# Four v tiles first, projections in independent pairs, and parts of LN moved to GpSimd, in a fused attention and token-MLP kernel

## The chip, the cores and the metric

The kernel runs on one core of one Trainium2 chip. The time is the device time of one execution in microseconds (us), as a median of several executions. Most executions of one kernel agree within about 1 us (the kernel before took 178.03 to 179.87 us over all rounds; one execution in e6 fell into a slow state and took 217 us); more about that spread below. A profile is one execution with the hardware profiler on; its span (first to last instruction) is about 1.7 us shorter than the time. Names of engines in the profile: PE is TensorE's matmul side, PEld its weight loads, DVE is VectorE, ACT is ScalarE, POOL is GpSimd, SP is the engine that issues most DMAs. "PEclk" is the share of TensorE's full clock that the throttle granted.

## The reference, cut to what matters

Two branches of the same sequence (2048 tokens, 448 features) are mixed by a gate.

```python
def _layernorm(x, axis=-1, eps=1e-05):
    m = jnp.mean(x, axis=axis, keepdims=True)
    v = jnp.var(x, axis=axis, keepdims=True)
    return (x - m) / jnp.sqrt(v + eps)

# branch A: 16 heads of 28; q, k, v = x @ wq, x @ wk, x @ wv; 4 segments of 512 tokens, causal
# attention inside a segment, a linear memory (elu+1 features) over earlier segments; then @ wo
# branch B, a token MLP:
h = _layernorm(x)                                   # 16 tiles of 128 tokens x 448
u = gelu(einsum('bsd,sf->bdf', h, w1) + b1)         # f = 1792
y = einsum('bdf,fs->bds', u, w2) + b2
out = g * a + (1 - g) * y.transpose(0, 2, 1)        # g = sigmoid((x * gate_w).sum(-1))
```

## The kernel before

The program is one straight list of operations. Each has a name, its reads and writes, and possibly an alternative engine; a table `ORDER` fixes which engine runs it and in which order. Semaphores are derived from the reads and writes. Every engine works strictly down its own list, so an operation that is late holds up all that stand behind it.

The names used below: `trx0_*` are TensorE transposes of the first x tiles and `xTcp*` their copies out of PSUM; `v01a` to `d`, `k0`, `q0`, ... are projections; `padk*`, `padq*` copy wk and wq into a padded layout; `sc0_0` is a group of score matmuls, `exp0_0` its exponential on ScalarE, `mask0_*` its causal mask on GpSimd; `pv0` multiplies the first masked probabilities with v; `u0-5` is the matmul of hidden tile 0 with x tile 5, so it waits for `ln5`; `y15` is the last output tile.

```python
def ln_coef(t):                       # one call for 4 tiles
    t4 = slice(t, t + 4)
    op("DVE", lambda e: e.tensor_scalar_add(vpe[:, t4], mv[:, t4, 1], 1e-5), ...)               # variance + eps
    op("POOL", lambda e: e.tensor_tensor(rstd[:, t4], vpe[:, t4], mhalf[:, t4], op=ALU.pow), ...)  # ** -0.5
    op("DVE", lambda e: e.scalar_tensor_tensor(nmr[:, t4], mv[:, t4, 0], -1.0, rstd[:, t4],
                                               op0=ALU.mult, op1=ALU.mult), ...)                # -mean * rstd

def ln_apply(t):                      # 128 x 448, bf16, in place
    op("DVE", lambda e: e.tensor_scalar(xh[:, t, :], xh[:, t, :], rstd[:, t : t + 1], nmr[:, t : t + 1],
                                        op0=ALU.mult, op1=ALU.add), ...)                        # x * rstd + nmr

# project(): four outputs a, b, c, d; each pair shares the array as two half-row tiles
a, b, c, d = outs
R_h = Res(name, psum=True)            # ties the four parts together
ab = part(name + "a", (run(a, 0, True), run(b, 1, True)), ())
cd = part(name + "b", (run(c, 0, True), run(d, 1, True)), ())
part(name + "c", (run(b, 0, False), run(a, 1, False)), ()).deps.append(ab)
part(name + "d", (run(d, 0, False), run(c, 1, False)), uses).deps.append(cd)
...                                   # cut
ORDER = {"PE": """ warm fill0 gtr ... trx0_1 fill5 ... v01a v01b v01c v01d k0a k0b k0c k0d q0a ... sc0_4 pv0
                   u0-0 u4-0:2 u0-1:2 u1-0 ... y15-13 y12-10:4 """,            # cut
         "POOL": """ id0 z3_0 id1 v0 z3_1 mhalf v1 mask0_0_0 rstd0 rstd8 mask0_1_1 mask0_1_3 mask0_2_2
                     mask0_2_2~2 rstd4 maskg0 rstd12 ... """}                   # cut
```

## Time and profile before

The median was 178.05 us. What matters:

| | before |
|---|---|
| span of the profile | 176.6 us |
| useful matmuls, estimate from start-to-start distances (189 ns per 448 columns, 216 ns per pair of 512) | 157.4 us |
| first useful matmul / last one ends | 6.54 / 173.66 us |
| pv0 starts | 26.93 us |
| one LN apply on VectorE | 0.39 us |

First the page's lines of busy time and of the granted clock in 40 slices. PE is the engine with the least room, and it is dense from the second slice to the last; GpSimd has plenty.

```profile
span 176.6 us, 3765 instructions
PE 169.1 (96%) x1460; PEld 81.9 (46%) x1468; DVE 150.7 (85%) x332; ACT 128.8 (73%) x159; POOL 67.3 (38%) x93
...
PE   8899899999999999999999989999999999999993
...
PEclk9999999999999999999999999999999999999999
```

The chain of waits that ended last, by engine, is mostly TensorE itself:

```profile
PE 72%; DVE 15%; ACT 6%; DMA 2%; issue 1%; SPq 1%; POOL 1%; ACTq 0%
```

### The profile page before, as it was taken

Reading aid. Unit: us, or ns where it says so; the run is one execution under the profiler, and the core shown is the slowest. Engines: PE = TensorE matmul, PEld = TensorE weight load, DVE = VectorE, ACT = ScalarE, POOL = GpSimd, SP = SyncE. Lnnn points to the kernel's source line nnn. Section 1 sums busy time; section 2 is a strip of 40 time slices with the busy share of each in tenths; the row PEclk is TensorE's granted clock in tenths of the full one; section 3 lists DMA queues with packets and bytes.
Section 4 is the critical chain, followed back from the end, with each engine's and each line's share of the span. In section 5 each row is a group of like instructions: output and inputs, shape, how many; then the busy total and the mean of one; then the engine's idle time right before and its main releaser. Section 6 shows DMA issues by size and latency. Waiting matters only on the chain.

```text
span 176.6 us, 3765 instructions
## 1 busy us (share of the span) xinstructions
PE 169.1 (96%) x1460; PEld 81.9 (46%) x1468; DVE 150.7 (85%) x332; ACT 128.8 (73%) x159; POOL 67.3 (38%) x93
## 2 busy tenths in 40 slices
PE   8899899999999999999999989999999999999993
PEld 2654244443444444454444544444544445555561
DVE  0689999999988999998999898999999998994204
ACT  2559998889997899989999999997476795001100
POOL 7000853263153700383170560089527765220000
PEclk9999999999999999999999999999999999999999
DMA  5999992328899429922136450012910591909012
GB/s 146 347 273 315 290 233 44 84 59 227 144 245 258 118 61 277 261 11 43 28 80 167 102 151 0 7 30 66 264 41 0 176 265 36 280 6 266 20 52 78
DMA packets 49729, 24.51 MB, mean 139 GB/s; under 512 B 14240, under 2 KB 49472, under 8 KB 49712
## 3 DMA queue, kind: packets, MB, share of 16 engines
q1 hardware_dynamic: 49560, 24.16, 54.5%
q8 instruction: 11, 0.18, 0.4%
q10 hardware_dynamic: 152, 0.12, 0.2%
q14 instruction: 6, 0.05, 0.1%
HBM read 18.76 MB, written 2.36 MB: 120 GB/s over the span
## 4 chain that ended last, share of the span: by engine, by line
PE 72%; DVE 15%; ACT 6%; DMA 2%; issue 1%; SPq 1%; POOL 1%; ACTq 0%
PE t L1071 25%; PE t L672 15%; PE t L1042 14%; PE t L1022 7%; PE t L934 6%; ACT t L943 4%; PE t L971 4%; DMA t<-in_A_wk_dram 2%; DVE t L893 2%; PE t L820 2%; DVE t L708 1%; ACT t L1046 1%; DVE t L1054 1%; DVE t L754 1%; DVE t L779 1%
## 5 line engine op out<-in xcount | busy, mean ns | idle before, releaser
L943 ACT ACTIVATE t<-t 128x2048 bf16<-128x2048 f32 x40 | 75.1, 1876 | 7.9 <-PE t L934 7.7
L946 POOL TENSOR_SCALAR_AFFINE_SELECT t<-t 128x512 bf16<-128x512 bf16 x64 | 44.4, 714 | 51.8 <-ACT t L943 51.2
L1042 PE MATMUL t<-t 128*128 128x448 bf16 x224 | 46.9, 353 | 0.3
L1071 PE MATMUL t<-t 128*128 128x448 bf16 (+2 forms) x238 | 46.5, 342 | 0.2
L672 PE MATMUL t<-t 64*128 64x512 bf16 (+3 forms) x336 | 34.8, 350 | 2.5 <-DVE t L720 0.7
L1071 PEld LDWEIGHTS t<-t 128*128 128x128 bf16 x238 | 21.7, 98 | 20.4 <-issue 2.5
L1042 PEld LDWEIGHTS t<-t 128*128 128x128 bf16 x224 | 20.2, 98 | 21.4 <-issue 3.4
L1002 POOL TENSOR_TENSOR t<-t 128x448 bf16<-128x448 f32 x12 | 14.5, 1210 | 33.5 <-DVE t L998 15.4
L672 PEld LDWEIGHTS t<-t 64*128 64x128 bf16 x336 | 17.4, 94 | 17.4 <-DVE t L877 1.3
L1028 ACT ACTIVATE t<-t 128x448 bf16<-128x448 f32 x11 | 8.0, 728 | 17.5 <-PE t L1022 17.5
L1076 DVE SCALAR_TENSOR_TENSOR t<-t 128x448 bf16<-128x448 f32 (+2 forms) x17 | 10.7, 640 | 8.4 <-PE t L1071 8.3
L934 PE MATMUL t<-t 28*128 28x512 bf16 (+3 forms) x256 | 15.8, 301 | 0.6 <-ACT t L943 0.4
L1022 PE MATMUL t<-t 128*128 128x448 bf16 x64 | 14.4, 353 | 0.1
L1008 DVE STREAM_TRANSPOSE t<-t 128x512 bf16<-128x512 bf16 x16 | 11.0, 693 | 0.5 <-POOL t L1002 0.4
L934 PEld LDWEIGHTS t<-t 28*128 28x128 bf16 x256 | 4.4, 92 | 14.9 <-ACT t L943 7.7
L987 DVE STREAM_TRANSPOSE t<-t 128x512 f32<-128x512 f32 x16 | 11.0, 699 | 0.3 <-PE t L971 0.2
L971 PE MATMUL t<-t 128*32 128x512 bf16 (+3 forms) x256 | 10.9, 301 | 0.0
L1059 DVE SCALAR_TENSOR_TENSOR t<-t 128x448 bf16<-128x448 f32 x14 | 9.2, 664 | 1.2 <-ACT t L1057 1.1
L1046 ACT ACTIVATE t<-t 128x448 f32<-128x448 f32 x14 | 8.9, 638 | 1.7 <-PE t L971 1.0
L877 DVE BATCH_NORM_STATS2 t<-t 128x6 f32<-128x448 bf16 x16 | 9.6, 613 | 0.3 <-DMA t<-in_A_x_dram 0.3
L1054 DVE SCALAR_TENSOR_TENSOR t<-t 128x448 f32<-128x448 f32 x14 | 9.2, 665 | 0.0
L998 DVE SCALAR_TENSOR_TENSOR t<-t 128x448 f32<-128x448 f32 x12 | 8.9, 740 | 0.1
(77 smaller groups left out, 184.8 us busy)
## 6 DMA issues: line engine op xcount, KB each, us to landing
t<-in_B_w_dram SPq DMA_DIRECT2D x7, 1024.0 KB, 6.6
t<-in_B_w_dram SPq DMA_DIRECT2D x8, 896.0 KB, 5.5
out_dram<-t SPq DMA_DIRECT2D x15, 112.0 KB, 4.4
t<-in_A_x_dram SPq DMA_DIRECT2D x3, 448.0 KB, 5.0
t<-in_A_wo_dram SPq DMA_DIRECT2D x4, 98.0 KB
t<-in_A_wv_dram SPq DMA_DIRECT2D x1, 336.0 KB, 4.1
t<-in_A_wk_dram SPq DMA_DIRECT2D x1, 336.0 KB, 4.1
t<-in_A_wq_dram SPq DMA_DIRECT2D x1, 336.0 KB, 4.5
```

Source lines behind the costliest of these rows:

```text
L672: last = e.matmul(bank(o["b"])[:, 0 : o["n"]], o["w"](r, c), o["x"](r, c), start=first, stop=end, skip_group_check=True)
L934: last = e.matmul(bank(hl)[:, c0 : c0 + w], kT[r, hg, s * 512 + j * 128 : s * 512 + j * 128 + 128], qT[r, hg, s * 512 + 128 * j : s * 512 ...
L943: op("ACT", lambda e: e.activation(pslot(g), ps[:, 0:4, :], ACT.Exp, scale=SCALE), reads=R_bank[0:4], writes=[g.res], take=g, name=f"exp{p ...
L946: op("POOL", lambda e, c0=c0: e.affine_select(pslot(g)[:, :, c0 : c0 + 128], pslot(g)[:, :, c0 : c0 + 128], pattern=[[0, 4], [1, 128]], co ...
L971: last = e.matmul(bank(cb)[32 * hl : 32 * hl + 32, 128 * j : 512], vaug[:, 4 * s + j, 32 * h : 32 * h + 32], pslot(P_fill[u // 2][f])[:, h ...
L987: dv(lambda e: e.transpose(t2[:, 0, :], bank(cb)[:, 0:512]), [bres(cb)], [R_tt[tb][0]], "ta", 630, use=(cb,))
L1002: op("POOL", lambda e: e.tensor_tensor(o3, n3[0], n3[1], op=ALU.add), reads=R_tt[tb], writes=[R_ob[tb]], name=f"o{u}", cost=1280, port=Tru ...
L1008: dv(lambda e: e.transpose(oT[:, hg, s * 512 : s * 512 + 512], o), [R_ob[tb]], qres(hg, s), "ot", 635)
L1022: last = e.matmul(bank(b)[:, 0:D], oT[:, hg, T * 128 : T * 128 + 128], wo_sb[:, hg, :], start=(hg == 0), stop=(hg == NHG - 1), skip_group_ ...
L1042: op("PE", lambda e, st=st: e.matmul(bank(b)[:, 0:D], w1c[:, st, f2 * 128 : f2 * 128 + 128], xh[:, st, :], start=(st == 0), stop=(st == NT ...
L1054: op("DVE", lambda e: e.scalar_tensor_tensor(gg[:, q, :], gg[:, q, :], 1.0, vh[:, q, :], op0=ALU.add, op1=ALU.mult), reads=[R_gg[q], R_vh[ ...
L1071: op("PE", lambda e, ft=ft: e.matmul(bank(b)[:, 0 : c1 - c0], w2c[:, ft, t2_ * 128 : t2_ * 128 + 128], uT[:, ft, c0:c1], start=(ft == 0), ...
```

## The change

Its intent: fill TensorE's early wait for the padded wk with work that needs only wv (four whole v tiles instead of two in halves); load wv in three pieces, so that the first matmuls need only two of them; let pairs of outputs finish independently; and relieve VectorE in the crowded first 40 us by giving 8 of 16 LN applies, the small pads and the addition of eps to GpSimd. LN becomes subtract-multiply, which saves the small `nmr` instruction. All engines get a new order, and the warm-up matmuls are fewer.

```diff
-    load_w(lambda: wvx, WV, R_wv, "wv", ("SP", "SP"))
+    op("SP", lambda e: e.dma_start(wvx[:, 3, 0:D], WV[320:448]), writes=[R_wv[0]], name="ldwv0", ...)
+    for k, c, n in ((1, 0, 1), (2, 1, 2)): ...            # chunk 0, then chunks 1 and 2
-    warm_up(7, "warm", -1)                                # and NFILL = 9
+    warm_up(5, "warm", -1)                                # and NFILL = 6
+        for k in range(0, len(outs), 2):                  # project(): independent pairs
+            a, b = outs[k : k + 2]
+            whole = run(a, 0, True), run(b, 1, True)
+            if cut and k == 0:                            # the part that needs two pieces of wv only
+                part(name + "s", [seq[0:2] for seq in whole], (), R_wv[0:2])
+                whole = [seq[2:] for seq in whole]
 ... (cut)
     def ln_coef(t):
-        op("DVE", ... tensor_scalar_add(vpe[:, t4], mv[:, t4, 1], 1e-5) ...)
-        op("POOL", ... rstd = vpe ** -0.5 ...)
-        op("DVE", ... nmr = mean * -1.0 * rstd ...)
+        op("POOL", lambda e: e.tensor_scalar(rstd[:, t4], mv[:, t4, 1], 1e-5, None, op0=ALU.add), ...)
+        op("POOL", ... rstd = rstd ** -0.5 ...)
     def ln_apply(t):
-        op("DVE", lambda e: e.tensor_scalar(xh[:, t, :], xh[:, t, :], rstd[:, t : t + 1], nmr[:, t : t + 1],
-                                            op0=ALU.mult, op1=ALU.add), ...)
+        def fn(e):
+            return e.tensor_scalar(xh[:, t, :], xh[:, t, :], mv[:, t, 0:1], rstd[:, t : t + 1],
+                                   op0=ALU.subtract, op1=ALU.mult)
+        op("DVE", fn, ..., alt=("POOL", fn, pool_cost(448)))
 ... (cut) ORDER, GpSimd's list:
+        ... padx1 padk1 padq1 padq0 vpe0 rstd0 padq3 ln0 mask0_0_0 ln2 vpe4 rstd4 mask0_1_1
+        ln4 ln6 ln1 mask0_1_3 mask0_2_2 mask0_2_2~2 ln5 mask0_3_0 maskg0 vpe8 rstd8 mask0_4_1 ln7 vpe12 rstd12 ln10 ...
 ... TensorE's list ends with the 128-column half of y15 instead of y12-10:4:
-        ... y15-13~2 y15-13 y12-10:4
+        ... y14-13 y12-9:5 y15-0~2 ... y15-13~2
```

`pool_cost(448)` is the estimate for one LN apply on GpSimd; it gives 0.55 us.

## The prediction

> **What bounds the kernel.** TensorE. The page's busy line gives PE 96% of 176.6 us (VectorE 85%) at full granted clock, and the chain of waits that ended last is 72% PE. Matmul records carry latency (353 ns), so I took start-to-start distances on the timeline: 189 ns per 448-column matmul, 216 ns per 512-column pair of half-row projections. That makes 157.4 us of useful matmuls between 6.54 and 173.7 us, so about 9 us are not streaming. About half of those are changes of tiling: a matmul before a score group takes 285, not 189 ns. The Trainium skill, "TensorEngine Tiling (Array Packing)", Key Properties, says that a change of mode drains the array; this trace agrees, some 0.1 us each. Both orders have nearly as many changes (96 and 94), so that half stays.
>
> **What the change can reach.**
> 1. *Start.* v01 begins at 6.54 us, after ScalarE's second copy of transposed x (ends 6.46) and the last wv piece (lands 6.41). ScalarE's x tile is now issued 0.25 us earlier and only half of wv is needed first: -0.2 us.
> 2. *k0.* Before: v01 is used up at 7.9 us and k0 starts at 8.63, because the padded wk is ready only then (0.74 us lost). Now four v tiles come first, 14 pairs x 0.19 = 2.7 us, until about 9.0; wk lands about 0.6 us later than its 7.3 us because wv goes first; padk0 (0.55 us) and padx0 (0.2 us) follow, so k0 can start at about 9. Work due anyway fills the gap: -0.6 us.
> 3. *14 to 24 us.* Stalls before sc0_0, around the bias transpose and before k1 and q1 sum to 1.6 us, waits for evacuations by a VectorE busy with statistics. Pairs release banks after two outputs instead of four, statistics start near 3.5 instead of 6.8 us, and some 4 us of VectorE work go to GpSimd (8 of 16 LN applies at 0.3 us, small pads 1.0 us, eight 0.08 us coefficient instructions). I expect half: -0.8 us.
> 4. *Middle, 27 to 150 us.* Dense, with about 1.8 us of single stalls: -0.2 us, either sign.
> 5. *Tail.* The last matmul is followed by a 448-column final (0.68 us) and its 112 KB store, landing 2.4 us after it; after the change by 128 columns (0.35 us) and 32 KB: -0.5 us.
>
> **What it adds.** GpSimd, idle from 4 to 17.7 us, gets pads and LN applies. An LN apply there should take 0.6 us (a 512-column mask takes 0.64), but masks next to VectorE's two-input float operations took 0.93 to 1.1 us. The Trainium skill, "GPSIMD Engine Reference", Specifications, tells of SBUF interfaces shared with VectorE; those masks agree. LN applies precede masks in GpSimd's order, so pv0 may come up to 1 us late.
>
> **Sum.** About -2.3 us: 175.7 us, range 173.9 to 177.3. Faster by over 2%: 0.18, within 2%: 0.79, slower by over 2%: 0.03.
>
> **What would show it.** First v matmul near 6.3 us; no gap before k0; four v tiles done by 9.1; fewer PE gaps between 13 and 24 us; LN applies on GpSimd of 0.6 to 1.0 us; pv0 about 1 to 2 us earlier than 26.9; span after the last matmul 2.4 instead of 2.9 us.
>
> **What would make it wrong.** wk or wq landing over 1 us later; GpSimd LN over 1.2 us, delaying masks and u0; a later full clock, as there is less warm-up; the new order paying elsewhere in the dense middle.

## More of the kernel before

The group of all LN applies, with its columns: line, engine, operation, tiles, shapes, count, then busy us and mean ns of one, then idle time before them.

```profile
L893 DVE TENSOR_SCALAR t<-t 128x448 bf16<-128x448 bf16 x16 | 5.7, 389 | 0.1
```

And TensorE's timeline (start us, length us, engine, line, operation, shapes, count, idle time before and what ended it) around pv0, line L971. There is no gap ahead of it, and the first MLP matmuls (L1042) follow at once.

```profile
26.60 0.40 PE L934 MATMUL t<-t 28*128 28x384 bf16 x8
26.93 0.73 PE L971 MATMUL t<-t 128*32 128x512 bf16 x16
27.59 3.58 PE L1042 MATMUL t<-t 128*128 128x448 bf16 x18
```

## The result, and the profile after

The changed kernel took 183.64 us (183.27 to 184.42 in 4 runs) against 178.1 us for the kernel before in the same rounds: slower by 3.1% (ratio 1.0307, 95% interval 1.026 to 1.0354). Ratios here and below are the mean time of one kernel's fast runs over that of the other's of the same rounds, so they are not quite the ratios of the medians.

The lines that answer to those of before:

```profile
span 182.7 us, 3702 instructions
PE 170.8 (94%) x1435; PEld 80.5 (44%) x1435; DVE 148.2 (81%) x313; ACT 127.4 (70%) x153; POOL 83.8 (46%) x110
...
PE   7799980998999999999999999999999999999994
...
PEclk9999999699999999999999999999999999999999
...
PE 63%; POOL 12%; ACT 9%; DVE 8%; DMA 3%; issue 2%; SPq 2%; ACTq 0%
```

There is a hole in PE's row: a slice of 0 around 28 to 32 us. Right after it the granted clock dips, and GpSimd has gone from 1% to 12% of the chain that ended last. The group of LN applies on GpSimd, then its timeline and TensorE's at the hole:

```profile
L894 POOL TENSOR_SCALAR t<-t 128x448 bf16<-128x448 bf16 x8 | 15.2, 1902 | 0.0
```

```profile
24.08 0.63 POOL L949 TENSOR_SCALAR_AFFINE_SELECT t<-t 128x512 bf16<-128x512 bf16 x1
24.71 5.55 POOL L894 TENSOR_SCALAR t<-t 128x448 bf16<-128x448 bf16 x3
30.22 1.93 POOL L949 TENSOR_SCALAR_AFFINE_SELECT t<-t 128x512 bf16<-128x512 bf16 x3
```

```profile
25.63 1.47 PE L678 MATMUL t<-t 64*128 64x512 bf16 x12
32.20 1.26 PE L974 MATMUL t<-t 128*32 128x512 bf16 x16 [5.11 <-POOL t L949]
33.39 0.61 PE L937 MATMUL t<-t 28*128 28x384 bf16 x8
33.94 2.50 PE L1045 MATMUL t<-t 128*128 128x448 bf16 x8
```

One LN apply on GpSimd takes 1.90 us, not 0.6. Three of them in a row (`ln4 ln6 ln1`, 5.55 us) stand in front of the three masks that pv0 needs. TensorE idles for 5.11 us until the last of them is done. Then the throttle halves its clock: in a view by stretches, 26.3 to 32.2, 32.2 to 35.6 and 35.6 to 42.4 us, with the columns length, busy us and instructions of each engine, granted clock, DMA share and GB/s:

```profile
26.30:32.20 5.90, 0.80 (x8) 0.21 (x4) 2.94 (x9) 2.42 (x4) 5.83 (x7) 1.00 0.98 212
32.20:35.60 3.40, 3.40 (x29) 1.32 (x30) 1.41 (x3) 1.55 (x1) 3.32 (x5) 0.50 0.15 45
35.60:42.40 6.80, 6.15 (x40) 2.41 (x37) 4.69 (x16) 4.83 (x7) 6.71 (x7) 1.00 0.08 29
```

From pv0's stall on, GpSimd is busy nearly all the time. Where the extra time is by the traces: the first u matmul starts at 33.94 instead of 27.59 us (+6.35), and the last matmul ends at 180.30 instead of 173.66 us (+6.64). So against the kernel before nearly all of it has been lost by 34 us. (Against e1 below, which has the change's own TensorE order, the two differences are 5.14 and 6.93 us: there, 1.8 us of the loss comes after 34 us.)

The head did not gain either. The last piece of wk landed at 9.51 us (before: 7.32), and k0 started at 10.27 us (before: 8.63):

```profile
9.53 0.69 DVE L620 COPY t<-t 128x1176 bf16<-128x1176 bf16 x2 [2.85 <-DMA t<-in_A_wk_dram]
```

### The profile page after: what moved, and what is told of

Its sections match the earlier page's. It is cut to its first block, busy times and chain, and to the rows that moved or that the text cites. A ratio compares the mean times of both kernels' runs of the same rounds, so it can differ in the third digit from the quotient of the medians.

```text
span 182.7 us, 3702 instructions
## 1 busy us (share of the span) xinstructions
PE 170.8 (94%) x1435; PEld 80.5 (44%) x1435; DVE 148.2 (81%) x313; ACT 127.4 (70%) x153; POOL 83.8 (46%) x110
## 4 chain that ended last, share of the span: by engine, by line
PE 63%; POOL 12%; ACT 9%; DVE 8%; DMA 3%; issue 2%; SPq 2%; ACTq 0%
PE t L1074 24%; PE t L678 11%; PE t L1045 10%; POOL t L894 7%; PE t L1025 7%; ACT t L946 5%; PE t L937 5%; PE t L974 4%; DMA t<-in_A_wk_dram 3%; POOL t L949 2%; POOL t L889 2%; ACT t L1049 1%; PE t L960 1%; ACT t L1060 1%; DVE t L1062 1%
## 5 line engine op out<-in xcount | busy, mean ns | idle before, releaser
L949 POOL TENSOR_SCALAR_AFFINE_SELECT t<-t 128x512 bf16<-128x512 bf16 x64 | 43.1, 691 | 51.3 <-ACT t L946 50.6
L1045 PE MATMUL t<-t 128*128 128x448 bf16 x224 | 48.0, 358 | 0.7 <-POOL t L894 0.6
L678 PE MATMUL t<-t 64*128 64x512 bf16 (+1 forms) x308 | 35.1, 367 | 2.1 <-DMA t<-in_A_wv_dram 0.8
L678 PEld LDWEIGHTS t<-t 64*128 64x128 bf16 x308 | 15.5, 94 | 19.3 <-issue 3.2
L1031 ACT ACTIVATE t<-t 128x448 bf16<-128x448 f32 x10 | 7.2, 727 | 16.1 <-PE t L1025 16.1
L974 PE MATMUL t<-t 128*32 128x512 bf16 (+3 forms) x256 | 11.4, 312 | 5.1 <-POOL t L949 5.1
L894 POOL TENSOR_SCALAR t<-t 128x448 bf16<-128x448 bf16 x8 | 15.2, 1902 | 0.0
L990 DVE STREAM_TRANSPOSE t<-t 128x512 f32<-128x512 f32 x16 | 11.0, 702 | 4.8 <-PE t L974 4.7
L1025 PE MATMUL t<-t 128*128 128x448 bf16 x64 | 14.2, 353 | 0.0
L974 PEld LDWEIGHTS t<-t 128*32 128x32 bf16 x256 | 5.7, 98 | 11.7 <-POOL t L949 5.8
L988 DVE STREAM_TRANSPOSE t<-t 128x512 f32<-128x512 f32 x12 | 8.5, 705 | 1.4 <-PE t L960 1.4
```

The lines of the kernel that those rows point to most:

```text
L678: last = e.matmul(bank(o["b"])[:, 0 : o["n"]], o["w"](r, c), o["x"](r, c), start=first, stop=end, skip_group_check=True)
L894: return e.tensor_scalar(xh[:, t, :], xh[:, t, :], mv[:, t, 0:1], rstd[:, t : t + 1], op0=ALU.subtract, op1=ALU.mult)
L949: op("POOL", lambda e, c0=c0: e.affine_select(pslot(g)[:, :, c0 : c0 + 128], pslot(g)[:, :, c0 : c0 + 128], pattern=[[0, 4], [1, 128]], co ...
L974: last = e.matmul(bank(cb)[32 * hl : 32 * hl + 32, 128 * j : 512], vaug[:, 4 * s + j, 32 * h : 32 * h + 32], pslot(P_fill[u // 2][f])[:, h ...
L990: dv(lambda e: e.transpose(t2[:, 0, :], bank(cb)[:, 0:512]), [bres(cb)], [R_tt[tb][0]], "ta", 630, use=(cb,))
L1025: last = e.matmul(bank(b)[:, 0:D], oT[:, hg, T * 128 : T * 128 + 128], wo_sb[:, hg, :], start=(hg == 0), stop=(hg == NHG - 1), skip_group_ ...
```

## The experiments

Theory A: the LN applies on GpSimd, at 1.9 us each, hold up masks and tiles; this costs the 6 us. Rival B: the new order of projections and loads costs it, since wk lands 2.2 us later. Rival C: less warm-up lowers the clock. Edits of `ORDER` are shown as the names that moved; everything unnamed is as in the kernel it starts from.

### e1_ln_dve: the 8 LN applies back on VectorE

```diff
 POOL: - ln0 ln2 ln4 ln6 ln1 ln5 ln7 ln10
 DVE:  ... cpq1_3 + ln0 ln1 ln2 ... cpq1_0 cpq1_2 + ln4 ln5 ... bna14 + ln6 ln7 ta0 ... ln9 + ln10 ...
```

> The changed kernel with one edit: its 8 LN applies on GpSimd are given back to VectorE, all else kept. Theory A (GpSimd's LN applies of 1.87 us each hold up the masks, so pv0 starts at 32.2 instead of 26.9 us and TensorE's granted clock drops while it waits): pv0 back to about 27.2, no stall of over 1 us before it, granted clock 1.00, time 177 to 178.5 us. Rival B (the new order of projections and loads, with wk landing 2.2 us later, is what costs): over 181 us, since those stay. Rival C (less warm-up lowers the clock): clock stays under 1.00.

Measured: 177.51 us, 0.9941 of the kernel before (0.9912 to 0.9971), with the clock at 1.00. The whole loss is gone, and the rest of the change is a small gain. pv0 started at 27.82 us; it now waited 1.26 us, for VectorE:

```profile
25.09 1.47 PE L680 MATMUL t<-t 64*128 64x512 bf16 x12
27.82 0.73 PE L976 MATMUL t<-t 128*32 128x512 bf16 x16 [1.26 <-DVE t L775]
```

Rivals B and C fall as causes of the loss: the order of projections and loads and the short warm-up are all still there (wk landed at 8.98 us). A's figure for pv0 was 0.6 us too good, because of that wait; its "no stall of over 1 us" was a miss too.

### e2_masks_first: the masks of pv0 ahead of five LN applies, all on GpSimd

```diff
 POOL: ... ln0 mask0_0_0 - ln2 vpe4 rstd4 mask0_1_1 - ln4 ln6 ln1 mask0_1_3 mask0_2_2 mask0_2_2~2
       + ln1 ln2 ln4 ln5 ln6 mask0_3_0 ...
```

> The changed kernel with GpSimd's order alone altered: the four masks that pv0 waits for go ahead of ln1, ln2, ln4, ln5 and ln6, which then follow one another. If it is only the place of the masks in GpSimd's order (theory A1): about 178 us, pv0 at about 27. If it is GpSimd's total work before the first MLP tiles (theory A2, 8 x 1.87 = 15 us): pv0 at about 27 but the u matmuls then wait for ln1 to ln6, ready every 1.9 us until about 36, and the time stays above 180.5 us.

Measured: 186.5 us, 1.0438 of the kernel before, so even slower than the change. pv0 starts at 27.36 us, but the u matmuls then wait for one LN apply after the other; the last line is of the view of all waits (us in total, times, longest us):

```profile
30.14 0.93 PE L1046 MATMUL t<-t 128*128 128x448 bf16 x4 [0.86 <-POOL t L895]
31.00 0.18 PE L855 MATMUL t<-t 30*128 30x30 bf16 x1
31.99 0.36 PE L1046 MATMUL t<-t 128*128 128x448 bf16 x1 [0.80 <-POOL t L895]
33.83 2.05 PE L1046 MATMUL t<-t 128*128 128x448 bf16 x5 [1.48 <-POOL t L895]
...
39.68 0.35 PE L1046 MATMUL t<-t 128*128 128x448 bf16 x1 [2.34 <-DVE t L860]
...
DVE t L895 <- POOL t L890: 8.9, 2, 7.6
```

The clock record of this run has two stretches of 3.4 us at half clock (from 33.5 and from 40.3 us) instead of one. The longest wait, 2.34 us, is for a small VectorE operation (L860), but it too goes back to GpSimd: VectorE had stood idle for 7.6 us until GpSimd, behind five LN applies, computed the `rstd` (L890) of the next four tiles. So it is not the place of the masks alone; 15 us of LN do not fit on GpSimd before the MLP starts. Moving the wait only broke it into pieces. Whether the second stretch at half clock adds to the 2.3% over the change was not tried.

### e3_forms: what one LN apply costs on GpSimd, in eight forms

```diff
 def ln_apply(t), on GpSimd:
+    ln0: tensor_scalar(x, mean, rstd, subtract, mult)      ln2: tensor_scalar(x, rstd, mean, mult, add)
+    ln4: tensor_scalar(x, 0.001, 1.5, subtract, mult)      ln6: tensor_scalar(x, rstd, mult)
+    ln1: as ln0, 224 columns     ln5: tensor_scalar(x, 1.5, mult)
+    ln7: tensor_copy(x)          ln10: tensor_tensor(x, x, mult)
```

> The changed kernel with its 8 LN applies on GpSimd written in 8 forms, with a wrong result on purpose, to measure what one costs: ln0 as is (1.87 us), ln2 multiply-add with two columns, ln4 subtract-multiply with two constants, ln6 multiply by one column, ln1 as is on 224 columns, ln5 multiply by one constant, ln7 a copy, ln10 a product of two tensors. If the cost is per element and per arithmetic step (theory): half the columns about 1.0 us, one step about 1.0 to 1.2, two constants no cheaper than two columns, copy about 0.6. If it is a fixed cost of fetching columns: 224 columns near 1.8 us and two constants about 0.6.

Measured, in the order ln0, ln4, ln6, ln5, ln1, ln10, ln2, ln7:

```profile
L909 POOL TENSOR_SCALAR t<-t 128x448 bf16<-128x448 bf16 x1 | 1.9, 1875 | 0.0
L898 POOL TENSOR_SCALAR t<-t 128x448 bf16<-128x448 bf16 x1 | 1.7, 1720 | 0.1
L900 POOL TENSOR_SCALAR t<-t 128x448 bf16<-128x448 bf16 x1 | 1.5, 1453 | 0.0
L904 POOL TENSOR_SCALAR t<-t 128x448 bf16<-128x448 bf16 x1 | 1.3, 1340 | 0.0
L902 POOL TENSOR_SCALAR t<-t 128x224 bf16<-128x224 bf16 x1 | 1.1, 1117 | 0.0
...
L908 POOL TENSOR_TENSOR t<-t 128x448 bf16<-128x448 bf16 x1 | 0.9, 932 | 0.0
...
L896 POOL TENSOR_SCALAR t<-t 128x448 bf16<-128x448 bf16 x1 | 0.7, 714 | 0.0
L906 POOL COPY t<-t 128x448 bf16<-128x448 bf16 x1 | 0.6, 588 | 0.0
```

The per-element part of the theory held: 224 columns fewer save 0.76 us, and constants save only 0.15 us against columns. What nobody expected is in the line before the last: multiply-add with two columns, the form that the kernel before used, took 0.71 us, less than half of a multiplication alone (1.45 us). Why is not shown. My own "one step 1.0 to 1.2 us" was too low. So the change did two things at once to LN: it moved half of the applies, and it rewrote all of them into a form that costs nothing on VectorE (0.39 us either way, the median of 16 in the kernel before and in e1) and 2.6 times as much on GpSimd. One record of each form is thin evidence; e5 gives eight.

### e4_before_tail: the kernel before with the change's ending

```diff
 PE:  - y15-0~2 ... y15-13~2 (in between)   ... y12-10:4 + y15-0~2 ... y15-13~2
 DVE: ... fin14 - fin15~2 fin15 fin12 + fin15~2      SP: ... out14 - out15~2 out15 out12 + out15~2
```

> The kernel before with one part of the change: at the end TensorE does the 128-column half of the last output tile last instead of the last four matmuls of tile 12; the VectorE and store orders follow. If the change's end is worth what I predicted: last matmul to end 2.4 instead of 2.9 us, time 0.4 to 0.6 us less than before. If another store or the closing barrier sets the end: same time.

Measured: 177.92 us, 0.9966 of the kernel before (0.9943 to 0.9989), about 0.6 us. From the last matmul to the end its trace has 2.4 us, where before has 2.9. This part of the change does what was predicted.

### e5_muladd: LN as multiply-add, still on GpSimd

```diff
 def ln_coef(t):
+    op("DVE", ... nmr = mean * -1.0 * rstd ...)
 def ln_apply(t):
-    tensor_scalar(x, mean, rstd, subtract, mult)
+    tensor_scalar(x, rstd, nmr, mult, add)
 DVE: + nmr0 after mk0_0, nmr4 after cpq1_3, nmr8 after bna13, nmr12 after mk0_1
```

> The changed kernel with LN again as multiply-add (x times rstd plus a prepared column), its 8 applies still on GpSimd, in the change's order; four small VectorE instructions of 0.08 us prepare the column. If the form of the arithmetic is the cause (0.71 us in one record of the forms run against 1.87): all 8 applies near 0.7 us, GpSimd busy 9 us less, pv0 at 27.5 to 28.5, clock 1.00, time 176.5 to 178.5. If GpSimd is simply too slow a place for LN: applies still over 1.2 us and time over 180.

Measured: 179.29 us, 1.0026 of the kernel before (0.9992 to 1.006). The ratio falls from 1.0307 to 1.0026, so the form alone returns about 5.0 of the 5.5 us, at the same place in the order and on the same engine:

```profile
L899 POOL TENSOR_SCALAR t<-t 128x448 bf16<-128x448 bf16 x8 | 6.1, 772 | 1.9 <-DVE t L893 1.9
```

Seven of the eight took 0.72 us, ln0 1.14 us. The time is 0.8 us above what I expected, though in these rounds the kernel before too was slower (median 178.96 us): pv0 started at 28.08 us and still waited for masks behind LN applies.

```profile
28.08 0.73 PE L979 MATMUL t<-t 128*32 128x512 bf16 x16 [1.60 <-POOL t L954]
```

### e6_evac, e7_loads, e8_xtcp: three repairs of the head, one on top of the other

All three start from e1.

```diff
 e6  DVE: ... bns14 + cpq1_0 cpq1_2 bna8 omgh bns9 ln3 - cpq1_0 cpq1_2 ln4 ln5 ...
 e7  SP:  - ldwv1 ldx0 ldx2 ldwv0 ldwk0 ldwv2 ldwq0 ldwk ldwq
          + ldx0 ldwv1 ldx2 ldwv0 ldwv2 ldwk0 ldwk ldwq0 ldwq
 e8  DVE: - bns0 bns1 gw ob0 xTcp0_00 xTcp0_10   + bns0 bns1 xTcp0_00 gw xTcp0_10 ob0
```

> The run with LN on VectorE, plus one move in VectorE's order: the evacuations of q1's two outputs go ahead of the statistics and the LN apply that stood before them. Theory: pv0 waited 1.4 us there for its bank, which that evacuation frees. Then pv0 starts about 1 us earlier (26.7 instead of 27.8) and the time falls by 0.8 to 1.2 us, to about 176.5. If the masks or the exponentials gate pv0, it moves by under 0.3 us.

Measured: three fast runs, 177.77 to 178.07 us, 0.9947 of the kernel before (0.9912 to 0.9982), so no gain over e1 (0.9941). Its profiled run (217.28 us, clock 0.757) is not read. The trace of e7, which contains the same edit and that of the loads, suggests why. The wait of pv0 is down to 0.23 us, and a new one of 1.49 us stands ten u matmuls later, for the VectorE transpose that frees pv0's bank:

```profile
26.13 0.73 PE L976 MATMUL t<-t 128*32 128x512 bf16 x16 [0.23 <-DVE t L775]
...
28.86 0.55 PE L1047 MATMUL t<-t 128*128 128x448 bf16 x2
30.90 0.92 PE L1047 MATMUL t<-t 128*128 128x448 bf16 x4 [1.49 <-DVE t L992]
```

VectorE with all 16 LN applies has no room there. What one evacuation gains, the next one loses. My theory that pv0's bank was worth 1 us was wrong as an isolated repair.

> The run before this one, plus the order of the first loads: first x tile first, the second half of wv before wk, and wk's large piece before wq's small one. Theory: the change put 448 KB of weights in other places of the one queue, so wk lands at 9.0 to 9.5 us and k0 waits for it. Then wv's second half lands about 0.4 us earlier, wk about 0.5 us earlier (8.5), k0 starts about 9.3 instead of 9.8, and the time falls by 0.3 to 0.5 us. If the x transposes that now follow directly take the bandwidth, wk's landing does not move.

Measured: 177.24 us, 0.9918 (0.9883 to 0.9952). wk landed at 8.32 us (e1: 8.98) and k0 started at 9.18 us (e1: 9.75). So a part of the late landing was the place in the queue, as expected. One landing is thin evidence, but all traces together point the same way, with some overlap: with the change's order of loads (the change, e1 to e3, e5, e6, e10) wk landed between 8.45 and 9.51 us, with e7's (e7 to e9, e11, e12) between 7.99 and 8.82 us. The ratio fell by 0.003 from e6's, but the intervals overlap.

> The run before this one, plus VectorE's copy of the transposed x ahead of the gate column and of a memset. Theory: v03 starts at 6.4 because that copy ends at 6.35; with it first, v03 starts at about 5.7, and then waits for wv's second half (about 6.4), so k0 and the time gain 0.3 us at most, or nothing if wk still sets k0.

Measured: 177.39 us, 0.9924 (0.9882 to 0.9966). No gain. In its profiled run, the slowest of the four, the full clock came only at 9.11 us and v03 started at 7.09 us, not 5.7, so what the edit does at an early start is not shown.

### e9_best: multiply-add on GpSimd with an order to fit

```diff
 (from the change, with e5's LN and e7's loads)
 POOL: ... rstd0 padq3 ln0 ln1 ln2 ln3 mask0_0_0 vpe4 rstd4 mask0_1_1 mask0_1_3 ln4 ln5 mask0_2_2 mask0_2_2~2
       ln6 ln7 vpe8 rstd8 mask0_3_0 maskg0 mask0_4_1 vpe12 rstd12 ln10 wo0 ...
 DVE:  xTcp0_10 + bns2 bns3 padk0 ...; cpv2 + nmr0; bns14 + cpq1_0 cpq1_2 bns9 bns11 bna8 bna10 bna9 bna11 ta0 omgh oc0 bna14
```

> A version meant to beat both: the changed kernel with LN as multiply-add, 9 of its applies on GpSimd but ln0 to ln3 in GpSimd's idle time before the first mask and pv0's masks ahead of ln6 and ln7; the loads in the order of the loads run; VectorE does the statistics of x tiles 2 and 3 while it waits for wk, evacuates q1 first, and takes the transpose that frees pv0's bank ahead of small work. Theory: the stalls before pv0 (0.4 to 1.8 us in the earlier runs) and at u0-5 (1.66 us) go together, since VectorE is relieved without GpSimd being late: pv0 at 26.0 to 26.6, u0-15 by 37, time 174.8 to 176.3 us, 1.2 to 1.8% faster than before. If the TensorE order of the change itself is what holds it, the time stays near 177.2.

Measured: 177.11 us, 0.9928 (0.9904 to 0.9951): better than before, but not by what I expected. By start-to-start distances its trace has stalls of 0.53 us before u4-0 (bank of the bias transpose) and 0.63 us a little later. I took the second for u0-10 and ln10. The trace says otherwise: u1-10, the first user of ln10, starts without a wait, and the stall stands three matmuls later before u1-12, for ln12 on VectorE. VectorE was late there: ln15, which started while GpSimd did ln10, took 1.41 us, where e11, without ln10 on GpSimd, has 0.40. (In the change itself four of VectorE's eight applies took 0.62 to 0.80 us, beside GpSimd's; in the kernel before none took over 0.40. So a part of the work that stayed on VectorE took longer too, which the prediction had not booked; the cause was not tried.) Its profiled run (178.31 us, the slowest of six) got the full clock only at 9.9 us, and its v tiles ran at half speed until then.

### e10_keep: TensorE kept busy while it waits

```diff
 (from the change)
+ PE: 20 matmuls of 512 columns with no use, into pv0's bank, directly ahead of pv0
```

> The changed kernel, where TensorE does 20 matmuls of no use (about 4.3 us) while it waits for pv0's masks, to keep the granted clock up. It measures what the lowered clock costs by itself: pv0 and the u matmuls after it run at full speed (u at 189 instead of 374 ns), granted clock 1.00. Since GpSimd's chain to ln10 (ready at 42.4 us) still gates u1-10, I expect only 0.3 to 0.9 us of the 5.5 us back. If the clock is the larger part of the loss, over 2 us come back.

Measured: 183.93 us, 1.0286 of the kernel before (1.026 to 1.0312), against 1.0307 for the change: 0.4 us less, well inside the intervals. In the traces the last matmul ends 0.2 us earlier (180.07 instead of 180.30 us). So my 0.3 to 0.9 us is neither shown nor refuted; over 2 us did not come back. The clock did stay up. In the same stretch in which the change had 0.50:

```profile
32.20:35.60 3.40, 3.40 (x38) 1.59 (x31) 1.41 (x3) 2.40 (x2) 3.32 (x5) 1.00 0.16 49
```

The u matmuls ran at 189 ns, reached the next operands earlier, and waited there: up to 42.3 us the trace has waits of 0.82 us (a VectorE operation), 0.63 and 0.65 us (GpSimd's LN applies), against one of 0.65 us in the change. So the half clock is a symptom that costs little or nothing here, as GpSimd's chain sets the pace either way.

### e11_vector, e12_warm: the last two

```diff
 e11 (from e9)   POOL: - ln10     DVE: ta0 + b1c b2c ...; bna13 + bns12 bna12 ...; ln8 + ln10
 e12 (from e11)  - warm_up(5), NFILL = 6   + warm_up(6), NFILL = 7      PE: ... fill5 + fill6 v03s ...
```

> The version that beat both, with three small moves: the two copies that free the bank of the bias transpose directly after the transpose that frees pv0's bank, ln10 on VectorE instead of GpSimd, and the last batch of statistics a little earlier. Theory: the stalls of 0.53 us before u4-0 and 0.63 us before u0-10 in its trace wait for just these. Then both stalls fall under 0.2 us and the time falls by 0.7 to 1.1 us, to about 176.2. If VectorE has no room there, the stalls move elsewhere and the time stays within 0.3 us of 177.1.

Measured: 176.49 us, 0.9871 (0.9838 to 0.9905). The stall before u4-0 is gone and the second is down from 0.63 to 0.41 us, not under 0.2 us as expected. If the move of ln10 helped, then by way of VectorE (see e9), and not because TensorE waited for ln10; the three moves were not tried apart.

> The same with one more warm-up matmul at the start and one more filler before v03 (6 and 7 instead of 5 and 6; the kernel before has 7 and 9). The traces show the full clock granted between 4.4 and 9.9 us of different executions, and where it came at 9.9 us the first v tiles ran at half speed. If the change's shorter warm-up makes that late grant more frequent, the slow executions (over 0.8 us above the median) become rarer and the full clock comes by 7 us in the trace; the median moves by under 0.3 us. If the phase of the clock's window alone decides, the spread stays.

Measured: 176.43 us, 0.9867 (0.9838 to 0.9895), six runs from 176.27 to 176.84 us. Its profile:

```profile
span 174.5 us, 3710 instructions
PE 169.8 (97%) x1437; PEld 81.4 (47%) x1437; DVE 146.9 (84%) x317; ACT 127.0 (73%) x153; POOL 74.7 (43%) x110
```

With e11 it is the best version here, 1.3% faster than the kernel before and correct. Whether the added warm-up helps is open: e11's six runs lie between 176.18 and 177.17 us, and e12's profile has no clock record.

## Why the prediction was wrong

The forecast was 175.7 us; measured was 183.64 us. Point by point:

1. **GpSimd's LN apply (under "What it adds"): this step failed and decides the result.** I wrote "should take 0.6 us (a 512-column mask takes 0.64)". I took the duration of another instruction on the same engine for that of one which the trace before did not contain. It measured 1.90 us. Eight of them add 15.2 us to GpSimd where I had booked about 5. The path was foreseen: LN applies ahead of the masks, "so pv0 may come up to 1 us late"; at three times the cost it came 5.3 us late (32.20 instead of 26.93 us). The prediction named the case ("GpSimd LN over 1.2 us, delaying masks and u0") and gave it too little weight. e1 takes the applies away and recovers the loss; e5 changes only their form and recovers about 5.0 of 5.5 us; e2 shows that putting the masks first does not help.
2. **k0 (-0.6 us): failed.** I let wk land 0.6 us later than its 7.3 us. It landed at 9.51 us, and at 8.98 us in e1. It is issued 0.94 us later than before, and two more pieces (wv's first, wq's small one) stand before it. e7 moves it to 8.32 us by order alone. Why the rest is late was not tried. k0 started at 10.27 us, with two more v tiles done (1.3 us), so about 0.3 us was lost where I had booked a gain. In e1, with the same start but wk at 8.98 us, k0 started at 9.75 us: 0.2 us gained.
3. **Start (-0.2 us): nearly right.** v03 started at 6.41 us instead of 6.54, but it had four matmuls and then waited for wv's second half (0.77 us, landed at 7.59 us). Four tiles were done by about 10.2, not 9.1 us.
4. **14 to 24 us (-0.8 us): no gain shown.** In a fixed window of 14 to 24 us I counted fewer stalls in the change (1.2 against 1.6 us), but the work in it has shifted by 1.6 us. From the start of k0 to pv0, less the wait of pv0 itself, before takes 18.30 us; the change takes 16.82 us, with two v tiles (1.33 us) and the last score group (0.33 us) less in it. That is 18.5 us for nearly equal work.
5. **Middle (-0.2 us, either sign): open.** From the first u matmul to the last matmul before takes 146.1 us (27.59 to 173.66), e1 144.6 us (28.80 to 173.37), with the same work left. The waits of over 0.1 us in it sum to 1.3 us before and 0.5 us in e1. But e1 had paid 1.26 us just ahead of it, at pv0. e7, in the same TensorE order, pays 1.49 us inside instead and takes 146.0 us. So the new order can save about 1.5 us there, and does in e11 and e12 (144.8 us), but only if VectorE keeps up; the change by itself does not show it.
6. **End (-0.5 us): right.** 2.4 instead of 2.9 us after the last matmul, and e4 finds 0.6 us for it alone.
7. **The bound: right.** TensorE is the bound of the kernel before, and switches of tiling are a floor that stays. How the 9 us split is not settled: 96 changes at the prediction's own 0.1 us make 9.6 us, all of the 9 us and not half. The Trainium skill's drain at a change of mode (cited in the prediction) was not varied by any run; the trace's 285 against 189 ns is all there is.

In e1, where point 1 is away, the rest adds up: the first u matmul starts 1.2 us later than before, the middle is 1.5 us shorter, the end 0.55 us, and the span is 0.84 us shorter (the 0.6% gain). The prediction had -2.3 us for it. The sign of the result came from point 1.

On the Trainium skill: "GPSIMD Engine Reference", section 4.1, says of elementwise work on GpSimd that with one input it is "roughly line-rate". A copy of 448 columns took 0.59 us, subtract-multiply 1.88 us, where VectorE takes 0.39 us for the same LN apply. The measurement decides. "TensorE: Matmul & The Clock Gate", Part 1, tells of a half-rate clock after idle time and of a window of about 3.4 us; the trace agrees, with 0.50 for the 3.4 us from 32.2 us, after 5.11 us of idling.

## What to carry to other kernels

Before work moves to another engine, measure the exact instruction on that engine, in its exact form: here two ways to write the same LN cost the same on VectorE and differ by 2.6 times on GpSimd. An engine that is idle for half of the span (GpSimd: 54%) can still be the bottleneck of the 20 us in which everything behind it waits, so count its work in that stretch, in order, up to the first consumer. And when one wait is removed, look in the trace for the next one before booking the gain: e2 and e6 each removed a wait and e10 the half clock, and none gained more than the noise.

## What the Trainium skill lacked or had wrong

- "GPSIMD Engine Reference", section 4.1, calls one-input elementwise work on GpSimd roughly line-rate. For 448 bf16 columns the runs show 0.59 us for a copy and 0.72 us for multiply-add with two columns, but 1.88 us for subtract-multiply, 1.72 us for the same with constants, 1.45 us and 1.34 us for one multiplication. No page that I consulted tells that the pair of operations matters.
- The same page gives no cost of an instruction by form for `tensor_scalar`. Two sizes of subtract-multiply (1.117 us for 224 columns, 1.875 us for 448) make about 3.4 ns per column and 0.36 us fixed; this is my estimate from two records.
- "TensorE: Matmul & The Clock Gate", Part 1, speaks of the ramp as under 1% of a typical span and as varying from run to run. The runs agree (0.8 us of 177 us is 0.5%); what the page lacks is that this is as much as the gains one measures (e4: 0.6 us): the full clock came at 4.43 us in one profiled run of the kernel before and at 6.79 us in the run of e4, which has the same start, and the first v matmul began at 6.54 and 7.36 us, 0.8 us apart.
- "TensorE: Matmul & The Clock Gate", Terms, counts throttled time at a share K/N of the clock as a penalty of about that time × (1 − K/N). For the 3.4 us at 0.50 this would be 1.7 us (an estimate from the page's rule). Keeping the clock up gave back about 0.4 us, inside the noise (e10: ratio 1.0286 against 1.0307), because TensorE waited for another engine anyway.
